# Loading the first slice of a spatial weight before the stage that uses it, and a new pacing of the gating matmuls

## The chip, the cores and the metric

The kernel runs on one core of one Trainium2 chip. Its time is the device time of one execution in microseconds (us); the figure for a version is the median over several executions. The profile shows one execution: busy time and order of the engines (PE is TensorE for matmuls, PEld its weight loads, DVE is VectorE, ACT is ScalarE, POOL is GpSimd, SP is SyncE, which here only issues DMAs).

## The reference: an attention block and a gated MLP, mixed by a gate

S = 2048 tokens, D = 512, 32 heads of 16, a window of 256 tokens, FH = 896. Cut to what is computed:

```python
def _A_ref(x, wqkv, wo):                       # sliding-window attention
    q, k, v = split(x @ wqkv)                  # 32 heads of 16
    scores = einsum('bhqd,bhkd->bhqk', q, k) * 16 ** -0.5
    mask = (i - j >= 0) & (i - j < 256)
    p = softmax(where(mask, scores, -1e9))
    return merge_heads(p @ v) @ wo

def _B_ref(x, w_in, w_sp, b_sp, w_out):        # gMLP
    z = gelu(x @ w_in)
    z1 = z[..., :FH]
    z2 = layernorm(z[..., FH:])
    g = einsum('ts,bsf->btf', w_sp, z2) + b_sp[None, :, None]   # w_sp is 2048 x 2048
    return (z1 * g) @ w_out

g = sigmoid((x * gate_w).sum(-1))
return g * _A_ref(x, ...) + (1 - g) * _B_ref(x, ...)
```

The product with `w_sp`, called G below, needs `w_sp` transposed in on-chip memory, and it needs the normalized `z2`.

## The kernel before: the parts that matter here

The program is one stream of calls `R(engine, function, reads, writes)`; each engine runs its share in this order, and waits for the events of what it reads or overwrites. Stage 1 (0 to about 146 us) computes `z1`, `z2`, Q, K and V from x. Between the stages, every engine waits for every other. Stage 2 then interleaves three things on TensorE: attention, G and the output products.

The loads at the start and at the head of stage 2, with the normalization of `z2b` that stands between G and its input:

```python
# stage 1: w_o and w_out come early, they stay for the whole kernel
gW2.dma(lambda e: e.dma_start(wo_sb[:], A_wo...), writes=["wo"])
gW2.dma(lambda e: e.dma_start(wouth[:], B_w_out...), writes=["wouth"])
# ... stage 1 ...
sched.barrier_all()
# ... stage 2: two slots of the transposed spatial weight, 256 rows of w_sp each
wspT = SB("wspT", [128, 2, 16, 256], stack=s2)

def issue_wsp(n8):
    slot = n8 % 2
    for j in range(16):                        # 16 transposing DMAs for each slice n8
        grp.dma(lambda e, j=j: e.dma_start(wspT[:, slot, j, :],
            B_w_sp[256*n8:256*(n8+1), 128*j:128*(j+1)], transpose=True), ...)
# [cut]
issue_wsp(0)
issue_wsp(1)
ln_finalize_dve1()     # mean and variance of z2, on DVE
ln_finalize_act()      # square root on ACT, with its table
ln_finalize_dve2()     # 1/std, then 16 instructions: z2b[:, tt, :] normalized in place
```

G in 112 chunks: slice n8 (8 of them), 7 column tiles f7, each in two chunks of 8 matmuls; the second also adds the bias and lets DVE multiply the result into `z1T2`. When a slice is done, its slot is refilled with slice n8 + 2.

```python
def g_chunk_task(n8, f7, j0, j1, last, gbank):          # (j0, j1) is (0, 8) or (8, 16)
    for j in range(j0, j1):
        e.matmul(ps, z2b[:, j, f7*128:(f7+1)*128], wspT[:, slot, j, :], ...)   # 128x256
    if last:
        e.matmul(ps, ones4[r32:r32+1, :], bsp_rows[r32:r32+1, n8//4, :], ...)
    # [cut] then on DVE: z1T2 *= ps;  after f7 == 6: issue_wsp(n8 + 2)
```

The main loop: 16 query tiles t, 4 head groups g, and in each four steps of a score product and an exponential. After every step, `fill` puts in other TensorE work: queued items (probability times value, transposes, output products; each has a step before which it may not run), then chunks of G by a credit:

```python
for t in range(16):
    for g in range(4):
        for parity in range(2):
            for mp in range(2):
                scores_task(t, g, mp, parity)          # PE, into PSA
                exp_task(t, g, mp, parity, eslot)      # ACT, PSA -> E
                step_ctr[0] += 1
                fill(FILL_NS)                          # FILL_NS = 650
        mask_task(t, g, eslot)                         # POOL, in place on E
        enq(640, pv_half_task, ready_lag=4 or 5)       # PE, E x Vaug -> PSB
        # g == 3: enq(250, transpose_task), enq(1550, b_task), enq(900, a_task)

G_RATE = 480.0;  g_credit = [-4300.0];  G_CHUNK_EST = 950.0
def fill(budget_ns):
    used = 0
    while used < budget_ns:      # queued items that are ready
        ...
    while g_credit[0] >= 0:      # then chunks of G
        next_g_chunk();  g_credit[0] -= G_CHUNK_EST
    g_credit[0] += G_RATE

def b_task(t):                   # z1T2 x wouth
    while g_groups_done() < 7 * (t // 2 + 1):
        next_g_chunk()           # G that is not there yet is put in at once
```

Of the kernel before, what the change touches and what calls it, by code (L numbers as in the profile page):

```python
# [9 lines left out]
D = 512  # L10
# [98 lines left out]
def build_kernel(nc, A_x, A_wqkv, A_wo, B_w_in, B_w_sp, B_b_sp, B_w_out, gate_w, out, cfg=None):  # L109
    cfg = dict(cfg or {})  # L110
    taps = cfg.get("taps", {})
    do_stage2 = cfg.get("stage2", True)
# [4 lines left out]
    with gctx:  # L117
# [6 lines left out]
        dma_sem_pool = [sems[f"d{i}"] for i in range(20)]  # L124
# [11 lines left out]
        QTo = SB("QTo", [128, 4, 2048])  # L136
        KT = SB("KT", [128, 4, 2048])
        Vaug = SB("Vaug", [128, NT, H * 17])
        wo_sb = SB("wo_sb", [128, 4, D])
        wouth = SB("wouth", [128, 7, D])  # L140
        ident = SB("ident", [128, 128])
        ones4 = SB("ones4", [128, 128])
        bsp_rows = SB("bsp_rows", [128, 2, 256])
        consts = SB("consts", [128, 4], F32)
        g_sb = SB("g_sb", [128, NT], F32)
        omgh = SB("omgh", [128, NT], F32)
# [68 lines left out]
        for k in range(4):  # L215
# [5 lines left out]
                wqo[:, k, :].rearrange("p (m c) -> p m c", c=32)[:, :, 16:32],  # L221
                A_wqkv[k * 128:(k + 1) * 128, 0:512].rearrange("p (m c) -> p m c", c=32)[:, :, 16:32]),
                writes=[("wqo", k)])
        gW2 = new_dma_group(2)
        gW2.dma(lambda e: e.dma_start(wo_sb[:], A_wo.rearrange("(k p) c -> p k c", p=128)), writes=["wo"])
        gW2.dma(lambda e: e.dma_start(wouth[:], B_w_out.rearrange("(k p) c -> p k c", p=128)), writes=["wouth"])
        gB = new_dma_group(8)
        for n in range(8):
            gB.dma(lambda e, n=n: e.dma_start(
                bsp_rows[32 * (n % 4):32 * (n % 4) + 1, n // 4, :],  # L230
                B_b_sp[256 * n:256 * (n + 1)].rearrange("(o c) -> o c", o=1)),
                writes=[("bsp", n)])

        def z2_pe(j):
            tt, sp = j // 2, j % 2
# [253 lines left out]
        if do_stage2:  # L489
# [5 lines left out]
            OnT = SB("OnT", [128, 2, 4, 128], stack=s2)  # L495
            ostage = SB("ostage", [128, 2, 512], stack=s2)
            bh = SB("bh", [128, 2, 512], F32, stack=s2)
            wspT = SB("wspT", [128, 2, 16, 256], stack=s2)
            rec = SB("rec", [128, 2, 16], F32, stack=s2)

            wsem = [dma_sem_pool.pop(0), dma_sem_pool.pop(0)]
            osem = [dma_sem_pool.pop(0), dma_sem_pool.pop(0)]
            wuse = [0, 0]
            ouse = [0, 0]
            gated = set()
            state = dict(masked=set(), pv=set(), normed=set(), transposed=set(), ont=set(), scaled=set(),
                         exp=set())

            def issue_wsp(n8):
                slot = n8 % 2  # L510
                grp = _DmaGroup(sched, wsem[slot], 16, base=256 * wuse[slot])
                wuse[slot] += 1
                for j in range(16):
                    grp.dma(lambda e, j=j: e.dma_start(  # L514
                        wspT[:, slot, j, :], B_w_sp[256 * n8:256 * (n8 + 1), 128 * j:128 * (j + 1)],
                        transpose=True), writes=[("wspT", slot, j)])

            def g_chunk_task(n8, f7, j0, j1, last, gbank):
                assert ln_state.get("norm_done"), "G chunk before LN finalize"
                slot = n8 % 2  # L520
                ps = PSC[:, gbank, 0:256]

                def pe(e):
                    ins = None
                    for j in range(j0, j1):
                        ins = e.matmul(ps, z2b[:, j, f7 * 128:(f7 + 1) * 128], wspT[:, slot, j, :],  # L526
                                       start=(j == 0), stop=False)
                    if last:
                        r32 = 32 * (n8 % 4)
                        ins = e.matmul(ps, ones4[r32:r32 + 1, :], bsp_rows[r32:r32 + 1, n8 // 4, :],  # L530
                                       start=False, stop=True, tile_position=(r32, 0))
                    return ins
                rd = [("z2b", j) for j in range(j0, j1)] + [("wspT", slot, j) for j in range(j0, j1)]
                if last:
                    rd += ["ones4", ("bsp", n8)]
                R("pe", pe, reads=rd, writes=[("PSC", gbank)])
                if last:
                    def gt(e):
                        sl = z1T2[:, f7, 256 * n8:256 * (n8 + 1)]
                        return e.tensor_tensor(sl, ps, sl, ALU.mult)  # L540
                    R("dve", gt, writes=[("PSC", gbank), ("guT", f7, n8)])
                    gated.add((n8, f7))
                    if f7 == 6 and n8 + 2 < 8:
                        issue_wsp(n8 + 2)

            gq = [(n8, f7) for n8 in range(8) for f7 in range(7)]
            GCH = [(0, 8), (8, 16)]
            gstate = dict(gi=0, ci=0)

            def next_g_chunk():  # L550
# [16 lines left out]

            peq = []
            step_ctr = [0]

            def enq(est, fn, ready_lag=0, min_ready=0):
                peq.append(dict(ready=max(step_ctr[0] + ready_lag, min_ready), est=est, fn=fn))

            G_RATE = cfg.get("g_rate", 480.0)
            g_credit = [cfg.get("g_credit0", -4300.0)]
            G_CHUNK_EST = 950.0

            def fill(budget_ns, allow_g=True):
                used = 0
                while used < budget_ns:  # L580
                    item = None
                    for idx, it in enumerate(peq):
                        if it["ready"] <= step_ctr[0]:
                            item = peq.pop(idx)
                            break
                    if item is None:
                        break
                    item["fn"]()
                    used += item["est"]
                while allow_g and g_credit[0] >= 0:  # L590
                    if not next_g_chunk():
                        break
                    g_credit[0] -= G_CHUNK_EST
                    used += G_CHUNK_EST
                g_credit[0] += G_RATE

            slot_buf = {}

# [155 lines left out]
                    grp.dma(lambda e: e.dma_start(out2d[t * 128:(t + 1) * 128, :], ostage[:, oslot, :]),  # L754
                            reads=[("ostage", oslot)], writes=[("out", t)])

            issue_wsp(0)
            issue_wsp(1)
            ln_finalize_dve1()
            ln_finalize_act()  # L760
            ln_finalize_dve2()

            FILL_NS = cfg.get("fill_ns", 650)
            SCORES_PAIR = cfg.get("scores_pair", False)
            SCORES_ADJ = cfg.get("scores_adj", False)
            PV_LAG = cfg.get("pv_lag", 4)
# [1 line left out]
            for t in range(NQ):  # L768
                for g in range(4):
                    eslot = ebuf_counter[0] % 3  # L770
                    ebuf_counter[0] += 1
                    ensure_slot_free(eslot)
                    slot_buf[eslot] = (t, g)
                    for parity in range(2):
                        if SCORES_PAIR:
                            scores_task(t, g, 0, parity, both=True)
                            exp_task(t, g, 0, parity, eslot)
                            exp_task(t, g, 1, parity, eslot)
                            step_ctr[0] += 2
                            fill(2 * FILL_NS)  # L780
                        elif SCORES_ADJ:
                            scores_task(t, g, 0, parity)
                            scores_task(t, g, 1, parity)
                            exp_task(t, g, 0, parity, eslot)
                            exp_task(t, g, 1, parity, eslot)
                            step_ctr[0] += 2
                            fill(2 * FILL_NS)
                        else:
                            for mp in range(2):
                                scores_task(t, g, mp, parity)  # L790
                                exp_task(t, g, mp, parity, eslot)
                                step_ctr[0] += 1
                                fill(FILL_NS)
                    mask_task(t, g, eslot)
                    pvlag = PV_LAG + (1 if g >= 2 else 0)
                    enq(640, (lambda t=t, g=g, s=eslot: pv_half_task(t, g, s, (0, 1, 2, 3, 4, 5, 6, 7))),
                        ready_lag=pvlag)
                    if g == 1 or g == 3:
                        half = g // 2
                        enq(0, (lambda t=t, half=half: norm_task(t, half)), ready_lag=pvlag)  # L800
                    if g == 3:
                        enq(250, (lambda t=t: transpose_task(t)), ready_lag=pvlag + 2,
                            min_ready=(40 if t == 0 else 0))
                        enq(1550, (lambda t=t: b_task(t)), ready_lag=pvlag + 4, min_ready=(42 if t == 0 else 0))
                        enq(900, (lambda t=t: a_task(t)), ready_lag=pvlag + 6, min_ready=(44 if t == 0 else 0))
            step_ctr[0] += 1000
            fill(10 ** 9)
            assert not peq
            assert gstate["gi"] == len(gq)
            if do_out:  # L810
# [9 lines left out]
def bass_gated_mix__sliding_block__mixer_gmlp__prompt_kernel(  # L820
    nc, A_x, A_wqkv, A_wo, B_x, B_w_in, B_w_sp, B_b_sp, B_w_out, gate_w, out,
):
    build_kernel(nc, A_x, A_wqkv, A_wo, B_w_in, B_w_sp, B_b_sp, B_w_out, gate_w, out)


# [26 lines left out]
```

The softmax here doesn't subtract the row's maximum and nothing guards it: scores larger than these inputs give would overflow.

## Time and profile before

| | before |
|---|---|
| time, median of 4 (lowest to highest) | 455.91 us (454.87 to 457.56) |
| span of the profiled execution | 454.0 us |
| mean granted TensorE clock | 0.938 |
| busy PE, ACT, DVE, POOL | 383.0, 284.5, 199.1, 178.5 us |
| stage 1, to the last projection | about 143 us |
| last chunk of G ends | about 407 us |

A row of the groups view reads: line of the kernel, engine, operation, output tile, input tiles, count; then busy time and mean duration; then the time that the engine stood idle just before these instructions, and what ended it. In the page's strip of 40 slices, a slice is 11.35 us long and a digit is the busy share in tenths; the row PEclk is the granted TensorE clock in tenths of full speed.

### The profile page before, as it was taken

Reading aid. Unit: us, or ns where it says so; the run is one execution under the profiler, and the core shown is the slowest. Engines: PE = TensorE matmul, PEld = TensorE weight load, DVE = VectorE, ACT = ScalarE, POOL = GpSimd, SP = SyncE. Lnnn points to the kernel's source line nnn. Section 1 sums busy time; section 2 is a strip of 40 time slices with the busy share of each in tenths; the row PEclk is TensorE's granted clock in tenths of the full one; section 3 lists DMA queues with packets and bytes.
Section 4 is the critical chain, followed back from the end, with each engine's and each line's share of the span. In section 5 each row is a group of like instructions: output and inputs, shape, how many; then the busy total and the mean of one; then the engine's idle time right before and its main releaser. Section 6 shows DMA issues by size and latency. Waiting matters only on the chain.

```text
span 454.0 us, 10814 instructions
## 1 busy us (share of the span) xinstructions
PE 383.0 (84%) x4632; PEld 226.2 (50%) x4632; DVE 199.1 (44%) x424; ACT 284.5 (63%) x445; POOL 178.5 (39%) x191
## 2 busy tenths in 40 slices
PE   0499999999995219989999999999999999998774
PEld 0133434334342016747576666666666766754531
DVE  0057878787777702333243334234234333342322
ACT  1068777777786505746376775776766766767850
POOL 5033333333332103335154544544544554545550
PEclk9999999999998558999999999999999999996766
DMA  8990000000000222122121121221222210000000
GB/s 173 278 143 20 1 1 1 1 1 1 2 0 0 52 52 49 43 48 66 25 50 48 32 47 42 49 47 31 43 48 51 47 36 3 13 13 3 13 13 12
DMA packets 67663, 18.14 MB, mean 40 GB/s; under 512 B 62616, under 2 KB 67104, under 8 KB 67616
## 3 DMA queue, kind: packets, MB, share of 16 engines
q1 hardware_dynamic: 67616, 17.46, 17.0%
q8 instruction: 36, 0.59, 0.5%
q14 instruction: 11, 0.09, 0.1%
HBM read 4.85 MB, written 2.10 MB: 15 GB/s over the span
## 4 chain that ended last, share of the span: by engine, by line
PE 67%; ACT 14%; SPq 6%; DVE 4%; issue 3%; DMA 3%; POOL 1%; POOLq 0%; ACTq 0%; DVEq 0%
PE PSC L526 19%; PE PSB L672 9%; PE PSA L626 9%; PE PSC L357 8%; ACT E L639 7%; PE PSB L729 7%; PE PSB L300 6%; SPq L514 4%; ACT sq L307 4%; PE PSB L744 3%; PE PSC L367 3%; DMA w_in_sb<-in_B_w_in_dram 2%; SPq L199 2%; PE PSC L530 2%; PE PSB L707 1%
## 5 line engine op out<-in xcount | busy, mean ns | idle before, releaser
L639 ACT ACTIVATE E<-PSA 128x768 bf16<-128x768 f32 (+2 forms) x256 | 184.8, 771 | 105.7 <-PE PSA L626 102.6
L526 PE MATMUL PSC<-wspT,z2b 128*128 128x256 bf16 x896 | 118.4, 276 | 14.5 <-DMA wspT<-in_B_w_sp_dram 14.4
L649 POOL TENSOR_SCALAR_AFFINE_SELECT E<-E 128x1024 bf16<-128x1024 bf16 x56 | 61.2, 1093 | 128.6 <-ACT E L639 128.6
L526 PEld LDWEIGHTS PSC<-wspT,z2b 128*128 128x128 bf16 x896 | 80.6, 98 | 33.5 <-issue 14.8
L653 POOL TENSOR_SCALAR_AFFINE_SELECT E<-E 128x1024 bf16<-128x1024 bf16 x64 | 70.0, 1094 | 40.1 <-ACT E L639 27.4
L540 DVE TENSOR_TENSOR z1T<-PSC,z1T 128x256 bf16<-128x256 f32 x56 | 23.7, 424 | 82.9 <-PE PSC L530 76.3
L626 PE MATMUL PSA<-QTe,KT 32*128 32x128 bf16 x720 | 42.0, 223 | 8.8 <-ACT E L639 4.8
L672 PE MATMUL PSB<-Vaug,E 128*128 128x17 bf16 x1440 | 46.9, 172 | 2.7 <-POOL E L653 2.7
L626 PE MATMUL PSA<-QTo,KT 32*128 32x128 bf16 x720 | 41.7, 225 | 8.4 <-ACT E L639 8.3
L266 POOL TENSOR_SCALAR v<-sq 128x448 bf16<-128x448 bf16 x32 | 23.3, 728 | 60.6 <-ACT sq L258 60.6
L672 PEld LDWEIGHTS PSB<-Vaug,E 128*128 128x128 bf16 x1440 | 40.8, 97 | 9.8 <-POOL E L653 3.3
L307 ACT ACTIVATE sq<-PSB 128x512 bf16<-128x512 f32 x28 | 16.7, 597 | 42.4 <-PE PSB L300 42.3
L315 DVE TENSOR_TENSOR in<-PSB,v 128x512 bf16<-128x512 f32 x28 | 19.4, 691 | 41.8 <-POOL v L313 41.7
L626 PEld LDWEIGHTS PSA<-QTe,KT 32*128 32x128 bf16 x720 | 21.1, 94 | 24.1 <-issue 13.4
L357 PE MATMUL PSC<-xT,wk 128*128 128x512 bf16 x64 | 16.9, 412 | 18.4 <-DMA wv<-in_A_wqkv_dram 16.4
L729 PE MATMUL PSB<-wouth,z1T 128*128 128x512 bf16 x112 | 31.1, 424 | 1.6 <-DVE bh L733 0.6
L626 PEld LDWEIGHTS PSA<-QTo,KT 32*128 32x128 bf16 x720 | 20.9, 94 | 21.5 <-ACT E L639 19.1
L300 PE MATMUL PSB<-xT,w_in_sb 128*128 128x512 bf16 x112 | 30.0, 392 | 1.2 <-DMA w_in_sb<-in_B_w_in_dram 1.2
L313 POOL TENSOR_SCALAR v<-sq 128x512 bf16<-128x512 bf16 x28 | 17.4, 621 | 34.6 <-ACT sq L307 34.5
L241 PE MATMUL PSA<-w_in_sb,xT 128*128 128x448 bf16 x128 | 30.2, 359 | 0.0
L733 DVE TENSOR_SCALAR bh<-PSB,omgh 128x512 f32<-128x512 f32 x16 | 12.0, 750 | 39.2 <-PE PSB L729 39.2
L690 DVE RECIPROCAL rec<-PSB 128x16 f32<-128x16 f32 x32 | 8.2, 258 | 43.1 <-PE PSB L672 43.1
(61 smaller groups left out, 408.9 us busy)
## 6 DMA issues: line engine op xcount, KB each, us to landing
wspT<-in_B_w_sp_dram SPq DMA_TRANSPOSE x128, 2.4
out_dram<-ostage SPq DMA_DIRECT2D x16, 128.0 KB, 1.9
w_in_sb<-in_B_w_in_dram SPq DMA_DIRECT2D x1, 1792.0 KB, 9.9
wouth<-in_B_w_out_dram SPq DMA_DIRECT2D x1, 896.0 KB, 5.9
wk<-in_A_wqkv_dram SPq DMA_DIRECT2D x1, 512.0 KB, 4.8
wv<-in_A_wqkv_dram SPq DMA_DIRECT2D x1, 512.0 KB, 5.6
wo_sb<-in_A_wo_dram SPq DMA_DIRECT2D x1, 512.0 KB, 4.5
wqe<-in_A_wqkv_dram SPq DMA_DIRECT2D x4, 64.0 KB, 3.9
```

Of the source, the lines that this page charges most:

```text
L241: ins = e.matmul(ps, xT[:, k, tt * 128:(tt + 1) * 128], w_in_sb[:, k, FH + 448 * sp:FH + 448 * (sp + 1)], start=(k == 0), stop=(k == 3))
L300: ins = e.matmul(ps, w_in_sb[:, k, f7 * 128:(f7 + 1) * 128], xT[:, k, n4 * 512:(n4 + 1) * 512], start=(k == 0), stop=(k == 3))
L307: R("act", lambda e: e.activation(sq1[:, i % 2, :], ps, ACTF.Square), writes=[("PSB", i % 2), ("sq1", i % 2)])
L357: ins = e.matmul(ps, wsb[:, k, g * 128:(g + 1) * 128], xT[:, k, n4 * 512:(n4 + 1) * 512], start=(k == 0), stop=(k == 3))
L526: ins = e.matmul(ps, z2b[:, j, f7 * 128:(f7 + 1) * 128], wspT[:, slot, j, :], start=(j == 0), stop=False)
L540: return e.tensor_tensor(sl, ps, sl, ALU.mult)
L626: ins = e.matmul(PSA[:, m, b * 128:(b + 1) * 128], KT[32 * m:32 * m + 32, g, kt * 128:(kt + 1) * 128], QTp[32 * m:32 * m + 32, g, t * 128: ...
L639: return e.activation(E[:, eslot, m0:m0 + 2, parity, c0:384], PSA[:, m0:m0 + 2, c0:384], ACTF.Exp, scale=0.25)
L649: R("pool", lambda e: e.affine_select(E8[:, eslot, :, 0:128], E8[:, eslot, :, 0:128], pattern=[[0, 8], [-1, 128]], compare_op=ALU.is_ge, f ...
L653: R("pool", lambda e: e.affine_select(E8[:, eslot, :, 256:384], E8[:, eslot, :, 256:384], pattern=[[0, 8], [1, 128]], compare_op=ALU.is_ge ...
L672: ins = e.matmul(PSB[:, obank, hc:hc + 17], E[:, eslot, m, parity, b * 128:(b + 1) * 128], Vaug[:, kt, Hh * 17:Hh * 17 + 17], start=(b == ...
L729: ins = e.matmul(PSB[:, 1, :], z1T2[:, f7, t * 128:(t + 1) * 128], wouth[:, f7, :], start=(f7 == 0), stop=(f7 == 6))
```

## The change

It does four things. Slot 0 of the transposed spatial weight becomes a tensor that lives through the whole kernel (`wspT0`), and slice 0 is loaded into it during stage 1. In exchange `wo_sb` and `wouth`, used only by the output products, move into stage 2 and are loaded there after slice 1. The pacing of G is rewritten: the credit starts at 0 in place of -4300, a chunk costs 910 at a rate of 455 per step, and queued items are no longer limited by a budget per step. The bias rows of `w_sp` are laid out on two partitions in place of four. The purpose is that G can begin as soon as stage 2 does, and is spread evenly over the steps.

```diff
-        wo_sb = SB("wo_sb", [128, 4, D])
-        wouth = SB("wouth", [128, 7, D])
+        wspT0 = SB("wspT0", [128, 16, 256])
-        bsp_rows = SB("bsp_rows", [128, 2, 256])
+        bsp_rows = SB("bsp_rows", [128, 4, 256])
@@ loads of stage 1
-        gW2 = new_dma_group(2)
-        gW2.dma(... wo_sb ...)
-        gW2.dma(... wouth ...)
         gB = new_dma_group(8)
         # [cut: bias rows to partitions 32 * (n % 2)]
+        wsp_tensors = [wspT0, None]
+        def issue_wsp(n8): ...          # as before, into wsp_tensors[slot]
+        if do_stage2:
+            issue_wsp(0)
@@ stage 2
-            wspT = SB("wspT", [128, 2, 16, 256], stack=s2)
+            wspT1 = SB("wspT1", [128, 16, 256], stack=s2)
+            wo_sb = SB("wo_sb", [128, 4, D], stack=s2)
+            wouth = SB("wouth", [128, 7, D], stack=s2)
@@ pacing; the launch sets g_rate to 455, NGCH is 2
-            G_RATE = cfg.get("g_rate", 480.0)
-            g_credit = [cfg.get("g_credit0", -4300.0)]
-            G_CHUNK_EST = 950.0
+            FILL_MODE = cfg.get("fill_mode", "credit")
+            G_CHUNK_EST = cfg.get("g_chunk_est", 110.0 * 16 / NGCH + (30.0))
+            G_RATE = cfg.get("g_rate", 440.0)
+            g_credit = [cfg.get("g_credit0", 0.0)]
+            def fill(used, target=None):
+                if FILL_MODE == "credit":
+                    while True:                    # every queued item that is ready
+                        ...
+                    while g_credit[0] >= 0:
+                        next_g_chunk();  g_credit[0] -= G_CHUNK_EST
+                    g_credit[0] += G_RATE
+                    return used
+                # [cut: another mode, not used]
@@ head of stage 2
-            issue_wsp(0)
+            wsp_tensors[1] = wspT1
             issue_wsp(1)
+            gW2 = new_dma_group(2)
+            gW2.dma(... wo_sb ...)
+            gW2.dma(... wouth ...)
             ln_finalize_dve1()
```

## The prediction

> **What bounds the kernel now.** I read the strip of slices first, to find where TensorE is not busy; then the busy times by stretch; then the order of time around the hole. TensorE works 84% of the span, and nearly all of its idle time is in three places: the start, slices 13 to 15, and the end.
>
> ```profile
> PE   0499999999995219989999999999999999998774
> ACT  1068777777786505746376775776766766767850
> PEclk9999999999998558999999999999999999996766
> ```
>
> The second place is the head of stage 2. By stretch (columns: stretch, its length, busy time of PE, PEld, DVE, ACT, POOL with the number of instructions, granted clock, share and GB/s of the DMA):
>
> ```profile
> 140.00:180.00 40.00, 16.86 (x171) 9.80 (x170) 18.27 (x46) 15.31 (x33) 7.01 (x7) 0.66 0.19 41
> ...
> 240.00:260.00 20.00, 19.74 (x296) 12.79 (x295) 6.71 (x14) 13.13 (x17) 10.89 (x10) 1.00 0.17 41
> ```
>
> In steady stage 2 PE is busy 19.74 of 20 us and ACT 13.13: TensorE bounds it, and what is removed from its waits comes off the end. In 140 to 180 us it is busy 16.86 of 40. Why, from the waits of PE and its order of time (start, length, line, tiles, count, and the idle time before with its releaser):
>
> ```profile
> PE PSC L526 <- DMA wspT<-in_B_w_sp_dram: 14.4, 1, 14.4
> ```
>
> ```profile
> 146.66 0.29 PE L626 MATMUL PSA<-QTe,KT 32*128 32x128 bf16 x4 [4.09 <-DVE omgh L430]
> 150.91 0.56 PE L626 MATMUL PSA<-QTo,KT 32*128 32x128 bf16 x4 [3.95 <-ACT E L639]
> ...
> 153.64 0.29 PE L626 MATMUL PSA<-QTe,KT 32*128 32x128 bf16 x4
> 168.31 1.87 PE L526 MATMUL PSC<-wspT,z2b 128*128 128x256 bf16 x8 [14.37 <-DMA wspT<-in_B_w_sp_dram]
> 170.10 0.29 PE L626 MATMUL PSA<-QTo,KT 32*128 32x128 bf16 x4
> 170.33 0.39 PE L672 MATMUL PSB<-Vaug,E 128*128 128x17 bf16 x8
> 170.56 1.87 PE L526 MATMUL PSC<-wspT,z2b 128*128 128x256 bf16 x8
> ```
>
> Ten score products are in, then the first chunk of G stands for 14.37 us until slice 0 has landed. The chain of waits shows the releaser's own delay: sixteen transposes issued by SP one after the other, the first at 146.61, the last at 164.48 and 1.24 us long, then 2.40 us to landing.
>
> ```profile
> 146.61 1.12 SPq L514
> ...
> 164.48 1.24 SPq L514
> 165.72 0.04 issue
> 165.77 2.40 DMA wspT<-in_B_w_sp_dram
> ```
>
> **The second gate behind the first.** G also needs the normalized z2b, and that is not moved. In DVE's order of time:
>
> ```profile
> 149.69 8.53 DVE L456 TENSOR_SCALAR z2b<-z2b,rstd,nmr 128x896 bf16<-128x896 bf16 x16
> ```
>
> It ends at 158.22. So no more than about 10 us of the hole can go, not 14.4 plus what stands before it.
>
> **What the Trainium skill says, and whether the trace agrees.** "TensorE: Matmul & The Clock Gate", Part 1, says that the array falls to half its clock after an idle window and returns after about 3.4 us of sustained work. The trace agrees: the granted clock is 0.50 in every stretch I asked for from 146 to 172 us, 0.85 in 172 to 174 and 1.00 after. A chunk of eight matmuls takes 1.79 us from its start to the next instruction when slow, and 0.98 when fast. "SBUF — State Buffer", section Terms, says that DVE and GpSimd share one pair of ports, held for a whole instruction, so the loser blocks. It agrees: of the 16 normalizations the median is 506 ns and one is 1400, and that one stands at 152.1 to 153.4, where POOL's first mask runs (152.14, 1.13 us). The same entry on the AXI fabric says that DMA and engines use separate ports; no run of the kernel before shows stage 1 with and without such a load, so that the early transposes cost stage 1 nothing is my reading of it, not a measurement.
>
> **The change, part by part.**
>
> *Early slice 0.* Its 16 transposes are issued behind the bias rows, whose issues end at 32.57 us (30.05 + 2.52), so they end near 32.6 + 16 x 1.285 = 53 us and land by 56. SP waits for the end of stage 1 until 146.6 us anyway. Stage 1 gains and loses nothing.
>
> *New order at the head.* I followed the two pacing loops by hand through all 256 steps. Before, chunks come after steps 10, 12, 14, ..., 24 of them by step 56, then four at once at step 57, because `b_task` of t = 2 needs 28; the last is at step 222. After, they come at steps 1, 3, 5, ..., 223, and none is forced. The queued items keep their steps, except one product at step 45 that moves to 44: the old budget of 650 was hardly ever used up. So the rewriting moves G nine steps forward and takes out one clump; from step 57 on the two programs are the same to within a step.
>
> *When the head is through.* Scores 0 at 146.66. Chunk 1 waits for z2b tiles 0 to 7. In the new order there is no mask before the fourth exponential, which stands behind chunk 2, so no normalization is blocked: 16 of them at a spacing of (8.53 - 0.51 - 0.9) / 15 = 0.475 us. Tile 7 is ready at 149.69 + 7 x 0.475 + 0.51 = 153.5, tile 15 at 157.3. Chunk 1 runs slow from 153.5 to 155.3, scores 1 and 2 follow, chunk 2 runs from 157.35 to 159.15, with the bias to 159.35. Before, this point was 172.36 + 0.22 = 172.6: 13.2 us earlier.
>
> *What is given back.* At 172.6 the old kernel had done 12 score steps and two probability products; the new one at 159.35 has done three steps. Nine steps of 0.12 us and two products of 0.32 us (from the chain, 0.23 for eight score matmuls to 0.22 for four, and 0.32) are 1.7 us. The clock: the old one turned fast 4.1 us after its first G matmul; the new one, with the 2 us hole before chunk 2, at about 157.35 + 4.1 = 161.45. The 2.1 us from 159.35 run at about half rate, which loses 1.0 us. In return the clump of step 57 goes, with the 0.52 us that PE waited there for DVE and 0.2 us between the groups, and a third of a microsecond at the end, where one exponential less follows the last chunk: 1.0 us.
>
> *The loads that move.* Slice 1 is issued from 146.6 to 167.2 and needed at step 29, which I estimate at 181 us from the count of matmuls. wo and w_out follow, 1.7 us of issue and 5.9 us to landing, so by 175; needed at step 41. Slice 2 is issued when slice 0 is used up, at step 27, near 179 us, lands near 203, and is needed at step 57, near 212. No wait, with 9 us the smallest margin.
>
> *Sum.* 13.2 - 1.7 - 1.0 + 1.0 = 11.5 us. I take off 0.5 for small waits of the tighter start (ACT has to follow scores that the old kernel had spread over an idle time), and predict 455.9 - 11.0 = 444.9 us, 2.4% less.
>
> **The rivals.**
>
> *The whole wait goes.* If normalization were not in the way, as in a reading of the waits alone, 14.4 us and the clump would go: 440.5 us. Against it stands the DVE row above. I give it 5%.
>
> *A late refill takes the place of the wait.* Slices need 20.6 us of issue, two go behind output stores on the same SP, and G now runs up to the refill sooner. If slice 2 or wo were late by 5 to 8 us, the time would be 450 to 453. For it: the margins are estimates. Against it: in the kernel before PE waits for this tile once only, and each slice has 28 steps of about 1.05 us to arrive. 8%.
>
> *ACT becomes the bound in the front part.* Before, ten exponentials ran beside the dead time; now all come behind 157 us. A step costs ACT 0.33 us at t = 0, against about 0.75 us of PE work, so it should keep up. If not, 2 to 3 us are lost: 447.5. 12%.
>
> *The tail moves.* After the last G chunk ACT paces the steps and the clock falls to 0.5 at times (0.71 in 420 to 440 us). Its phase can shift by a microsecond either way; that widens the range, but moves the middle little.
>
> **Range and chances.** Two percent less is 446.8 us, which leaves 1.9 us of my gain as a margin. The clock's phase at the head and in the tail (1 us each) and the spread of the times before (454.87 to 457.56) make the inner width; the second and third rival the upper side. So 442.9 to 448.0. Faster by over 2%: 0.83. Within 2%: 0.16, mostly from a gain of 7 to 9 us. Slower by over 2%: 0.01; nothing in the change adds work.
>
> **What would show it.** Right, if PE's wait for the transposed weight is gone and one near 6.6 us (146.9 to 153.5) plus one near 1.5 us stand there with DVE's normalization as their releaser; if all 16 normalizations take near 506 ns; if the clock is 1.00 from about 161.5; if the product of t = 2 starts near 212 in place of 223.10; and if the last chunk ends near 396. Wrong, if PE waits for `wspT0`, `wspT1`, `wo_sb` or `wouth`; if stage 1 ends later than 146.6; or if the steady spacing of 17.5 us for each t (240.80, 258.44, 275.99 in the chain) grows.

## The result and the profile after

The changed kernel takes 440.46 us (median of 11, 438.37 to 441.82), against 455.85 us for the kernel before (median of 15, 453.77 to 457.64): a ratio of 0.9658, 95% interval 0.9638 to 0.9679. It is 15.4 us faster, where I had predicted 11.0; the time lies below my range of 442.9 to 448.0. The direction and the main cause were right, the size was too small by 4.4 us.

In the changed kernel the lines have moved: L533 is G (was L526), L659 the scores (L626), L672 the exponential (L639), L705 the probability product (L672), L762 the output product b (L729), L470 the normalization (L456).

The strip of slices after, for the same three rows:

```profile
PE   0399999999999089999999999999999999989765
ACT  1067778777788436737667677676676675876840
PEclk9999999999999769999999999999999999996566
```

The hole of three slices has become one of about one. What PE waits for, from the list of waits (total, times, longest):

```profile
PE PSC L371 <- DMA wv<-in_A_wqkv_dram: 16.5, 1, 16.5
PE PSA L659 <- ACT E L672: 11.9, 33, 0.7
PE PSC L533 <- DVE z2b L470: 7.6, 2, 6.3
```

No wait for the transposed weight is left, and none has come for `wo_sb` or `wouth`. In its place stand two waits for the normalization, 7.6 us in all. PE's and then DVE's order of time at the head:

```profile
146.59 0.23 PE L659 MATMUL PSA<-QTe,KT 32*128 32x128 bf16 x2 [4.09 <-DVE omgh L444]
153.14 1.89 PE L533 MATMUL PSC<-wspT,z2b 128*128 128x256 bf16 x8 [6.32 <-DVE z2b L470]
...
156.52 1.89 PE L533 MATMUL PSC<-wspT,z2b 128*128 128x256 bf16 x8 [1.27 <-DVE z2b L470]
158.34 0.39 PE L537 MATMUL PSC<-bsp_rows,ones 1*128 1x256 bf16 x1
...
160.81 1.23 PE L533 MATMUL PSC<-wspT,z2b 128*128 128x256 bf16 x8
```

```profile
149.60 6.86 DVE L470 TENSOR_SCALAR z2b<-z2b,rstd,nmr 128x896 bf16<-128x896 bf16 x16
```

The shape is the one predicted: a wait of 6.3 us, one of 1.3, a slow clock for the first three chunks, and a fast one from within the fourth. The normalization is done in 6.86 us, not 8.53.

The starts of the output product b, once for each query tile, are a clock for the rest of stage 2. From the chain of work that ended last (start, length, what), first before (tiles 2 to 5, 7, 8 and 10 to 12), then after (tiles 2 to 5 and 10 to 12):

```profile
223.10 1.68 PE PSB L729 x7
240.80 1.62 PE PSB L729 x7
258.44 1.62 PE PSB L729 x7
275.99 1.62 PE PSB L729 x7
...
310.91 1.62 PE PSB L729 x7
328.32 1.62 PE PSB L729 x7
...
363.34 1.62 PE PSB L729 x7
382.03 1.62 PE PSB L729 x7
399.73 1.62 PE PSB L729 x7
```

```profile
209.11 1.62 PE PSB L762 x7
226.52 1.62 PE PSB L762 x7
243.92 1.62 PE PSB L762 x7
261.33 1.62 PE PSB L762 x7
...
348.36 1.62 PE PSB L762 x7
365.77 1.62 PE PSB L762 x7
383.18 1.62 PE PSB L762 x7
```

At tile 2 the new kernel leads by 14.0 us, at tile 12 by 16.55, at the end of the span by 15.3. So the lead is not made in the hole alone: a tile takes 17.41 us after, up to tile 11, where before it took 17.55 to 17.70 in tiles 2 to 4 and 18.69 in tile 10, which has nine chunks there in place of eight. I had said that from step 57 on the two programs are the same.

### The profile page after: what moved, and what is told of

Same layout as the page of the kernel before. It is cut to its first block, busy times and chain, and to the rows that moved or that the text cites. A ratio compares the mean times of both kernels' runs of the same rounds, so it can differ in the third digit from the quotient of the medians.

```text
span 438.7 us, 10808 instructions
## 1 busy us (share of the span) xinstructions
PE 376.6 (86%) x4632; PEld 223.2 (51%) x4632; DVE 199.9 (46%) x424; ACT 283.6 (65%) x445; POOL 178.4 (41%) x191
## 3 DMA queue, kind: packets, MB, share of 16 engines
q1 hardware_dynamic: 67616, 17.46, 17.7%
## 4 chain that ended last, share of the span: by engine, by line
PE 64%; ACT 18%; DVE 7%; issue 3%; SPq 2%; DMA 2%; POOL 1%; POOLq 0%; DVEq 0%; ACTq 0%
PE PSC L533 16%; ACT E L672 10%; PE PSB L705 9%; PE PSA L659 8%; PE PSC L371 8%; PE PSB L762 7%; PE PSB L314 6%; ACT sq L321 4%; PE PSB L777 4%; PE PSC L381 3%; SPq L198 2%; DMA w_in_sb<-in_B_w_in_dram 2%; DVE rec L724 2%; PE PSB L740 2%; DVE z2b L470 2%
## 5 line engine op out<-in xcount | busy, mean ns | idle before, releaser
L672 ACT ACTIVATE E<-PSA 128x768 bf16<-128x768 f32 (+2 forms) x256 | 183.8, 772 | 91.2 <-PE PSA L659 85.7
L533 PE MATMUL PSC<-wspT,z2b 128*128 128x256 bf16 x896 | 119.2, 277 | 7.6 <-DVE z2b L470 7.6
L533 PEld LDWEIGHTS PSC<-wspT,z2b 128*128 128x128 bf16 x896 | 82.1, 99 | 27.4 <-DVE z2b L470 7.9
L659 PE MATMUL PSA<-QTe,KT 32*128 32x128 bf16 x720 | 43.8, 224 | 12.9 <-ACT E L672 8.8
L705 PE MATMUL PSB<-Vaug,E 128*128 128x17 bf16 x1440 | 46.8, 171 | 2.4 <-POOL E L686 2.4
L659 PE MATMUL PSA<-QTo,KT 32*128 32x128 bf16 x720 | 43.7, 224 | 3.3 <-ACT E L672 3.1
L705 PEld LDWEIGHTS PSB<-Vaug,E 128*128 128x128 bf16 x1440 | 40.9, 97 | 9.6 <-POOL E L686 2.8
L659 PEld LDWEIGHTS PSA<-QTe,KT 32*128 32x128 bf16 x720 | 21.2, 94 | 33.5 <-ACT E L672 17.2
L762 PE MATMUL PSB<-wouth,z1T 128*128 128x512 bf16 x112 | 31.4, 427 | 0.5 <-DVE OnT L746 0.5
L659 PEld LDWEIGHTS PSA<-QTo,KT 32*128 32x128 bf16 x720 | 21.1, 94 | 6.4 <-ACT E L672 5.4
L282 DVE TENSOR_TENSOR in<-PSA,v 128x448 bf16<-128x448 f32 x32 | 19.9, 621 | 8.8 <-POOL v L280 8.8
```

The lines of the kernel that those rows point to most:

```text
L533: ins = e.matmul(ps, z2b[:, j, f7 * 128:(f7 + 1) * 128], wt[:, j, :], start=(j == 0), stop=False)
L659: ins = e.matmul(PSA[:, m, b * 128:(b + 1) * 128], KT[32 * m:32 * m + 32, g, kt * 128:(kt + 1) * 128], QTp[32 * m:32 * m + 32, g, t * 128: ...
L672: return e.activation(E[:, eslot, m0:m0 + 2, parity, c0:384], PSA[:, m0:m0 + 2, c0:384], ACTF.Exp, scale=0.25)
L705: ins = e.matmul(PSB[:, obank, hc:hc + 17], E[:, eslot, m, parity, b * 128:(b + 1) * 128], Vaug[:, kt, Hh * 17:Hh * 17 + 17], start=(b == ...
L762: ins = e.matmul(PSB[:, 1, :], z1T2[:, f7, t * 128:(t + 1) * 128], wouth[:, f7, :], start=(f7 == 0), stop=(f7 == 6))
```

## The experiments

My theory after the result: the early slice is worth about what I had worked out (12.2 us by the sum below), and the rest, 3.2 us, comes from the pacing, which I had valued at 1.0 us. The rivals: the load is the whole gain, 14.4 us and more; or the start of G at step 1 is. All times are medians, with the ratio to the kernel before on the same chip and its 95% interval; differences between versions are differences of medians.

**Loads of the change, pacing of before.**

```diff
-    cfg={'g_rate': 455.0}
+    cfg={'g_rate': 480.0, 'g_credit0': -4300.0, 'g_chunk_est': 950.0}
```

> The loads of the change with the pacing of the kernel before (credit from -4300, rate 480, 950 a chunk: chunks after steps 10, 12, 14, ..., four at once at step 57). Theory: the early slice gives the head of stage 2 and no more; chunk 1 then waits for the normalization only (near 154 us), chunk 2 to about 158.3, its bias ends near 160.3 with as many score steps done as before at 172.6, less 1 us for the slow clock: 455.9 - 12.2 = 443.7 us, and the pacing brings the other 3.2 us. All ten first scores stand before chunk 1, so POOL's first masks run beside the normalization and stretch it to about 8.5 us. Rival: the early load alone is the whole gain (the wait of 14.4 us plus what hung on it): 440.5 us.

Measured: 445.94 us, ratio 0.9776 (0.9756 to 0.9796). The rival falls: without the new pacing 5.5 us of the gain are missing. My 443.7 was missed as well, by 2 us. The starts of b show where: tiles 2 and 3 took 18.05 us each, slower than in the kernel before.

```profile
213.02 1.46 PE PSB L762 x6
231.07 1.46 PE PSB L762 x6
249.12 1.46 PE PSB L762 x6
```

One part of the change stood in this run and not in the kernel before, and I had passed over it: the bias rows on two partitions. (The budget per step for queued items is gone too, here and in the early slice alone below; by my count that moves one product by one step.) The normalization took 8.53 us, as expected: beside the first two masks, two of its 16 instructions took 1.28 and 1.41 us, where the median is 0.505.

**Pacing of the change, loads of before.** The bias rows and the budget per step for queued items also stay as before.

```diff
-            G_RATE = cfg.get("g_rate", 480.0)
-            g_credit = [cfg.get("g_credit0", -4300.0)]
-            G_CHUNK_EST = 950.0
+            G_RATE = cfg.get("g_rate", 455.0)
+            g_credit = [cfg.get("g_credit0", 0.0)]
+            G_CHUNK_EST = 910.0
```

> The kernel before with the new pacing alone (credit from 0, rate 455, 910 a chunk); slice 0 is still loaded at the head of stage 2. Theory: chunk 1 waits for slice 0 until 168.3 us with only three score steps done, so nine steps and two probability products come later (1.7 us), but the clump of step 57 and the even steps go (3.2 us): 454.4 us. Rival, pacing is worth nothing by itself: 457.6 us. Rival, the start at step 1 is what brings the gain: about 452 us or less.

Measured: 454.96 us, ratio 0.9976 (0.9957 to 0.9995). As expected: alone the pacing brings about 1 us. All score steps but the first now stand behind the late slice, a wait of 21.4 us in this run, where the kernel before has ten ahead of it. That this eats up the rest of what the pacing is worth is my reading; no run shows it by itself. Its tiles gave a second hint: 17.62 us during slices 2 and 3, 17.41 during 4 and 5, 17.62 again during 6 and 7, always at odd steps.

**G begun at step 9, with the clump of step 57.**

```diff
-    cfg={'g_rate': 455.0}
+    cfg={'g_rate': 455.0, 'g_credit0': -3640.0}
```

> The changed kernel with G begun at step 9 (credit from -3640): odd steps as in the changed kernel, but 24 chunks by step 56 and four at once at step 57; from step 58 on the order is the same as in the changed kernel. Theory: the head is worth the same either way, as the scores that come first fill the wait for the normalization; the clump costs 1.2 to 1.9 us: 441.7 to 442.4 us. Rival, starting at step 1 is itself the gain: 444 us or more. Rival, the clump is free: 440.5 us.

Measured: 443.17 us, ratio 0.9717 (0.9693 to 0.9741): 2.7 us over the changed kernel, more than the 1.2 to 1.9 expected. From tile 2 on it keeps 17.41 us, so the loss lies before. In the clump a chunk takes 1.15 us from the next, with the bias in it (205.65 to 207.95 for two), where a single one takes 0.98 to the scores behind it, and b waits 0.74 us for VectorE. ScalarE gets nothing meanwhile: it stands idle for 7.13 us there, and for 1.95 around the same b in the run without the clump further down.

```profile
205.65 2.15 PE L533 MATMUL PSC<-wspT,z2b 128*128 128x256 bf16 x16
207.74 0.28 PE L537 MATMUL PSC<-bsp_rows,ones 1*128 1x256 bf16 x1
207.95 2.15 PE L533 MATMUL PSC<-wspT,z2b 128*128 128x256 bf16 x16
210.03 0.28 PE L537 MATMUL PSC<-bsp_rows,ones 1*128 1x256 bf16 x1
211.06 1.24 PE L762 MATMUL PSB<-wouth,z1T 128*128 128x512 bf16 x5 [0.74 <-DVE z1T L547]
```

**Every chunk one step later.**

```diff
-    cfg={'g_rate': 455.0}
+    cfg={'g_rate': 455.0, 'g_credit0': -455.0}
```

> The changed kernel with every chunk one step later (credit from -455: steps 2, 4, ..., 224), no clump. Theory: a query tile takes 17.64 us where chunks stand at even steps (with the probability products) and 17.41 where they stand at odd ones, as the kernel before showed in its own even and odd parts; over about 13 tiles that is 2.4 to 3 us: 442.9 to 443.5 us. Rival, the place of a chunk within its pair of steps does not matter: 440.0 to 440.9 us.

Measured: 448.06 us, ratio 0.9832 (0.9807 to 0.9856). One step of shift costs 7.6 us, about three times what I expected: a tile takes 18.05 us. PE's order of time behind a second chunk, first in this run, then in the one below with the bias on other rows:

```profile
255.78 0.28 PE L537 MATMUL PSC<-bsp_rows,ones 1*128 1x256 bf16 x1
255.78 0.44 PE L659 MATMUL PSA<-QTe,KT 32*128 32x128 bf16 x6
256.16 0.77 PE L705 MATMUL PSB<-Vaug,E 128*128 128x17 bf16 x24
```

```profile
253.82 0.28 PE L537 MATMUL PSC<-bsp_rows,ones 1*128 1x256 bf16 x1
253.82 0.34 PE L659 MATMUL PSA<-QTe,KT 32*128 32x128 bf16 x6
254.09 0.76 PE L705 MATMUL PSB<-Vaug,E 128*128 128x17 bf16 x24
```

The six score matmuls after the bias matmul take 0.38 us to the next instruction in the first, and 0.27 in the second: 0.1 us for each column tile, four in a query tile.

**Even steps with the bias on partitions 64 and 96.**

```diff
-   bsp_rows[32 * (n % 2): ...];      r32 = 32 * (n8 % 2)
+   bsp_rows[64 + 32 * (n % 2): ...]; r32 = 64 + 32 * (n8 % 2)
    # and the credit from -455
```

> Chunks at the even steps 2, 4, ..., 224, with the bias rows on partitions 64 and 96. After an even step the scores of banks 0 and 1 follow, rows 0 to 63. Theory: with the bias off these rows a tile goes from 18.05 back to 17.64 us, 5 us in all: 443.1 us against 448.06 with the bias on 0 and 32. Rival, even steps are slow for another reason (the probability products stand beside the chunks): stays at 447.5 to 448.5 us.

Measured: 443.51 us, ratio 0.9714 (0.9684 to 0.9743), 17.63 us a tile. Of the 7.6 us of the even steps the rows of the bias were 4.6. The bias is a matmul of one row of the array; scores on the same half of the rows wait for it, scores on the other half do not. What remains of the even steps, 0.2 us a tile, I have not taken apart.

**Bias back on four partitions, the rest as changed.**

```diff
-   bsp_rows[32 * (n % 2): ...];  r32 = 32 * (n8 % 2)
+   bsp_rows[32 * (n % 4): ...];  r32 = 32 * (n8 % 4)
```

> The changed kernel with the bias rows back on four partitions (0, 32, 64, 96 by slice). Theory: a bias matmul on the same rows of the array as the score products right after it (banks 2 and 3, rows 64 to 127, after an odd step) holds them up by 0.05 us a time; so tiles during slices 2, 3, 6 and 7 take 17.62 us in place of 17.41, 1.4 us in all: 441.8 us. Rival, the layout of the bias is neutral, as the prediction silently had it: 440.0 to 440.9 us and 17.41 us in all tiles.

Measured: 439.95 us, ratio 0.9654 (0.9621 to 0.9688). The tiles did what I expected, 17.62 us during slices 2 and 3, 17.41 in the middle, 17.62 during 6 and 7, and from tile 2 to tile 12 it took 1.4 us longer (175.4 against 174.1). The whole time does not show it: the interval covers the changed kernel's. This run's last tiles, from tile 12 on, were 1.1 us shorter in the trace. At odd steps the scores are held up by the same 0.1 us (0.38 to the next instruction, for 0.27), but in two of the four column tiles PE's wait for ScalarE behind them is shorter by as much (0.23 for 0.33), so 0.21 us a tile is left of it. So the layout is real as a mechanism; at odd steps its effect on the total is too small for these runs.

**The early slice alone: loads of the change, pacing and bias of before.**

```diff
-    cfg={'g_rate': 455.0}
+    cfg={'g_rate': 480.0, 'g_credit0': -4300.0, 'g_chunk_est': 950.0}
     # and the bias on four partitions, as in the run above
```

> The early slice alone: loads of the change, pacing and bias rows of the kernel before. Theory: what the first run with the old pacing lost against 443.7 us was the bias on partitions 0 and 32 in its even steps; with four partitions tiles 2 to 4 take 17.64 us in place of 18.05, and the whole 1.4 us less than that run: 444.5 us. Rival, the bias had no part in it: 445.9 us.

Measured: 444.99 us, ratio 0.9752 (0.9729 to 0.9776). This parts the change: 11.0 us for the early slice (456.0 less 445.0), and 4.5 us for everything else (445.0 less 440.5). Tiles 2 and 3 are back from 18.05 us to 17.70 and 17.63; the whole is 1 us below the run with the bias on two partitions, which the intervals do not separate. The first score of stage 2 and b of tile 2 in this run:

```profile
145.20 0.24 PE L659 MATMUL PSA<-QTe,KT 32*128 32x128 bf16 x4 [4.08 <-DVE omgh L444]
...
211.49 1.69 PE L762 MATMUL PSB<-wouth,z1T 128*128 128x512 bf16 x7 [0.52 <-DVE z1T L547]
```

From the one to the other it takes 66.3 us, the kernel before 76.4 and the changed kernel 62.5. So 10.2 us of the early slice, and 3.8 us of the rest, lie ahead of tile 2.

**G begun at step 9 without the clump.**

```diff
-   (chunks by credit: steps 9, 11, ..., 55, and four at 57)
+   elif (st % 2 == 1 and st >= 9) or st in (22, 30, 38, 46):
+       next_g_chunk()
```

> As the run that begins G at step 9, but the four chunks that are missing by step 56 stand singly after steps 22, 30, 38 and 46, so that none is forced at step 57; all others at odd steps, the last at 223. It parts the 2.7 us that the late start with its clump lost against the changed kernel. If the clump was it: back to 440.5 to 441.2 us. If the late start was it (POOL's masks beside the normalization, the clock fast later): stays at 442.5 to 443.5 us. I expect about half each: 441.8 us.

Measured: 441.13 us, ratio 0.9673 (0.9649 to 0.9696). By the times the clump is the larger part, 2.0 us of the 2.7, and the late start is left with 0.7, which the intervals do not separate from nothing. By the traces the two are alike: from the first score of stage 2 to b of tile 2 the changed kernel takes 62.5 us, this run 63.7, and the one with the clump 64.8. So both cost something, and the split is not settled. The late start may also be the clock: it came to 1.00 at 14.6 us after the first score in the changed kernel, but at 17.8 in this run, 17.3 with the clump and 17.7 with the early slice alone. Some 3 us longer at a clock of 0.50 would by my estimate lose 1.5 us. In the first run, with G begun as late, it came at 15.0, so the order alone does not decide it.

**Seven chunks a tile.** The profile after showed something that neither kernel uses: once the last chunk of G is through, a tile takes hardly less time. By stretch (PE, PEld, DVE, ACT, POOL busy, clock):

```profile
365.77:383.18 17.41, 16.61 (x276) 11.56 (x277) 6.42 (x13) 12.11 (x16) 8.75 (x9) 1.00 0.03 9
383.18:399.40 16.22, 14.25 (x242) 9.49 (x243) 5.57 (x11) 12.10 (x16) 8.95 (x9) 0.92 0.03 10
399.40:415.88 16.48, 13.57 (x208) 7.63 (x209) 4.51 (x9) 12.00 (x16) 8.74 (x9) 0.60 0.03 10
```

Without a chunk a tile is only 0.9 us shorter, at a clock of 0.60. So G was stretched to the end:

```diff
-   while g_credit[0] >= 0: ...
+   if st >= 1000: ...                       # what is left, at the end
+   elif st % 2 == 1 and not (st >= 57 and st % 16 == 9):
+       next_g_chunk()
```

> The changed kernel with 28 chunks at the odd steps up to 55 as in the change, and from step 57 on seven chunks a tile in place of eight (odd steps, the one of the output product left out), so that the last comes at step 247 and not at 223. Theory: in the last tiles, where no chunk is left, TensorE waits for ScalarE and its clock falls, so a tile takes 16.2 to 16.5 us with hardly any G in it; with seven chunks in every tile it takes 17.41 - 1.06 = 16.35 us throughout: 12 tiles save 10.6 us: 429.9 us, and the granted clock stays at 1.00 to step 248. Rival, the matmuls are the same and TensorE bounds the stage, so the order changes nothing: 440 us. Rival, ScalarE's 12.1 us a tile plus its waits bound a tile at more than 16.35: 434 to 437 us.

Measured: 437.62 us, ratio 0.9600 (0.9571 to 0.9628). Better, but 8 us short of the theory. The clock stayed at 1.00 in the tiles with G; a tile took 17.16 us, not 16.35. Taking away a chunk of 1.06 us brought 0.25. Both my views of the bound were too simple: TensorE does not bound a tile alone, or the whole chunk would have gone, and neither does ScalarE with its 12.1 us.

**The same, with another chunk left out.**

```diff
-   elif st % 2 == 1 and not (st >= 57 and st % 16 == 9):
+   elif st % 2 == 1 and not (st >= 57 and st % 16 == 1):
```

> As the run with seven chunks a tile, but the chunk left out is the one beside a probability product (the odd step that is 1 modulo 16), not the one behind the output product. Theory: a tile is a chain of both engines, not TensorE alone: ScalarE can be at most two exponentials behind, and idles 0.89 us whenever a probability product and a chunk stand together between two score steps; taking the chunk away there takes about 0.8 us off a tile, whereas behind the output product it only made room for a wait of 0.56 us on VectorE: 16.6 us a tile and 437.6 - 12 x 0.55 = 431 us. Rival, where the chunk is left out does not matter: 437 to 438 us.

Measured: 432.38 us, ratio 0.9508 (0.9470 to 0.9546), 5.2 us below the run before it with the same number of chunks in every tile. Two tiles of it:

```profile
376.03:392.83 16.80, 15.88 (x266) 11.15 (x267) 6.18 (x12) 12.21 (x17) 8.74 (x9) 1.00 0.03 10
392.83:409.73 16.90, 15.97 (x266) 11.24 (x267) 6.61 (x13) 12.21 (x17) 8.72 (x9) 1.00 0.03 10
```

The place decides. ScalarE's order of time in a tile, first of the run that left out the chunk behind the output product, then of this one:

```profile
267.05 2.92 ACT L672 ACTIVATE E<-PSA 128x768 bf16<-128x768 f32 x4 [0.44 <-PE PSA L659]
270.86 2.92 ACT L672 ACTIVATE E<-PSA 128x768 bf16<-128x768 f32 x4 [0.89 <-PE PSA L659]
```

```profile
265.12 4.43 ACT L672 ACTIVATE E<-PSA 128x768 bf16<-128x768 f32 x6 [0.45 <-PE PSA L659]
269.74 1.51 ACT L672 ACTIVATE E<-PSA 128x768 bf16<-128x768 f32 x2 [0.18 <-PE PSA L659]
```

Where a probability product and a chunk stand together between two score steps, ScalarE runs dry for 0.89 us; with the chunk gone it works through. That ScalarE's wait is why the place decides is argued from these lines; the times show only that it does. This version beats both kernels: its median is 8.1 us below the changed one (ratios 0.9508 and 0.9658).

**Probability products at even steps only.** The output products move by one step with them.

```diff
-   pvlag = PV_LAG + (1 if g >= 2 else 0)
+   pvlag = PV_LAG + (2 if g >= 2 else 0)
    # seven chunks a tile, the step 13 modulo 16 left out
```

> Seven chunks a tile at odd steps (the step that is 13 modulo 16 left out), and all probability products at even steps (lag 6 in place of 5 for the groups 2 and 3), so that none stands beside a chunk; the output products move one step with them. Theory: with no piece longer than a chunk or an output product between two score steps, ScalarE's two idle times of 0.89 us in a tile both shrink to 0.3 or so: 16.0 to 16.4 us a tile and 425 to 429 us. Rival, TensorE itself needs about 15.8 us and the waits only move: 16.6 us a tile or more, 431 us and up.

Measured: 442.75 us, ratio 0.9718 (0.9690 to 0.9746). That is 14 to 18 us above what I expected. A tile took 17.33 us. With one long piece after nearly every score step, ScalarE got one exponential at a time in a part of each tile and waited before it:

```profile
264.31 0.81 ACT L672 ACTIVATE E<-PSA 128x768 bf16<-128x768 f32 x1 [0.67 <-PE PSA L659]
265.57 0.81 ACT L672 ACTIVATE E<-PSA 128x768 bf16<-128x768 f32 x1 [0.45 <-PE PSA L659]
267.45 0.81 ACT L672 ACTIVATE E<-PSA 128x768 bf16<-128x768 f32 x1 [1.07 <-PE PSA L659]
268.70 0.81 ACT L672 ACTIVATE E<-PSA 128x768 bf16<-128x768 f32 x1 [0.44 <-PE PSA L659]
270.53 2.22 ACT L672 ACTIVATE E<-PSA 128x768 bf16<-128x768 f32 x3 [1.02 <-PE PSA L659]
```

An even spread of the long pieces was the wrong aim. As I read it, the two score buffers want two score steps side by side, so that two exponentials are in stock before the next long piece; but the output products moved too, and no run parts the two.

## Why the prediction was wrong, point by point

*The bound and the hole: right for the hole.* What was taken from PE's wait came off the end. The early slice alone measured 11.0 us. My steps for the head, without the clump and the tail, were 13.2 - 1.7 - 1.0 = 10.5. But from "TensorE bounds it" I took that the order of the same matmuls costs nothing in steady stage 2, and that does not hold: the runs with seven chunks a tile differ by 5.2 us in the order alone.

*The second gate: right, and a little too late.* The normalization stands in the place of the weight, with waits of 6.32 and 1.27 us where I had 6.6 and 1.5. I took off one blocked instruction, 0.9 us, and that was a misreading: in the kernel before two stand beside masks, one of 1.28 us from 152.23 and the one of 1.40 from 153.44. Without both the 16 took 6.86 us, against my 7.6. The first two chunks of G were through at 158.56 (158.34 + 0.22), not 159.35: 0.8 us of gain. The clock was fast from about 161.3; I said 161.5. That is luck in part: I had counted 4.1 us from the second chunk, it was 4.7, and over all runs the clock came between 3.0 and 9.6 us after the first chunk. For b of tile 2 and the end of the last chunk I had said 212 and 396; they came at 209.11 and 391.

*The whole wait goes: wrong, although its 440.5 us is the time measured.* The waits for normalization are there, and the early slice alone does not reach it. That sum came out by chance.

*The loads that move: right.* No wait for any of them, so the rival of a late refill did not come true either, and the first score of stage 2 came at 146.59 against 146.66.

*The pacing: the step that failed.* I wrote that the rewriting "moves G nine steps forward and takes out one clump; from step 57 on the two programs are the same to within a step", and gave it 1.0 us. It measured 4.5 us, with all that the change does beside the loads. Most of it lies ahead of tile 2, 3.8 us by the traces. The parts, by the times: 2.0 us the clump, 0.7 the late start, and 1.8 (445.0 less 443.2) the odd steps with the bias rows.

- The clump: 0.7 us in the sum, 2.0 measured by the times and 1.1 by the traces. I counted PE's idle time beside it, and not that the four chunks themselves run at 1.15 us each with nothing for ScalarE to do.
- The start at step 1, which I had in the head alone: 0.7 us by the times, 1.2 by the traces, not separated from nothing nor from the chance of the clock.
- "To within a step" was an error in itself. A step's shift moves every chunk from one half of a score pair to the other: 17.41 us a tile at odd steps and 17.64 at even ones in the kernel before, for the tiles at steps 57 to 100 and 196 to 222. The kernel before showed this: its chain of b starts has both 17.64 and 17.41, and I quoted the spacing as one figure of 17.5.
- The bias layout, which I left out altogether. At odd steps it puts the bias off the rows of the next scores. Its share of the total here is at most 1.4 us and not separated from nothing; at even steps the same layout would have cost 4.6.

Counted by the traces from the start of the span, the lead at tile 2 is 14.0 us (10.7 by my steps and my discount of 0.5), then it grows by 2.6 to tile 12. Of that, 1.06 is a chunk that the kernel before has already done by then and the new one does later, which is most of the 1.3 us that the tail gives back. Differences of some tenths are within what one trace can vary: the first score of stage 2 came between 145.1 and 147.7 us in these runs.

*ACT as the bound in front: did not happen.* From 146.6 to 209.1 us PE waited for it 1.0 us in all.

*The range* was too narrow on the low side for one reason: I let all uncertainty of the pacing point upwards, towards waits, and none downwards.

## What to carry to other kernels

When a wait is removed, ask for the next gate behind it and work the new time out from that gate; this held here to within a microsecond. Where two engines alternate through two buffers, the order of the long pieces between the short ones can be a cost of its own, as the 17.16 and 16.80 us a tile with the same matmuls show: compare stretches of the old trace that differ only in that order before calling a re-pacing neutral. Spreading G to the last tiles, with the missing chunk taken from the better of the two places tried, gained another 8 us.

## What the runs showed that I had not expected

- A bias matmul of one row delays six score matmuls on the same half of the array by 0.1 us, and those on the other half not at all; at even steps this made 18.05 us a tile out of 17.63.
- TensorE's clock fell to 0.5 while PE was busy four fifths of the time with short matmuls. A stretch of the changed kernel's tail:

```profile
408.00:412.00 4.00, 3.10 (x63) 2.15 (x64) 0.00 (x0) 3.63 (x6) 2.19 (x2) 0.50 0.00 0
```

The output product at 415.8 took 3.17 us, against 1.69 at full clock.

- Beside the first two masks on POOL, two normalizations on DVE took 1.28 and 1.40 us in place of 0.51, in all five kernels that begin G at step 9 or 10 with the normalization still running (before, both with the loads alone, both late starts). In the changed kernel, where they do not meet, none did.
